# A fused attention and MLP kernel: the order of its first batch's steps, one chunk's place, and two loads moved

## The chip, the cores and the metric

The kernel runs on one core of one Trainium2 chip. The core has a matrix engine (PE), a vector engine (DVE), a scalar engine (ACT), GpSimd (POOL) and a fifth (SP) that here only issues DMAs. Each works through its own queue of instructions in order; semaphores tie the queues together. The metric is the time of one execution in microseconds, here the median of three runs.

## The reference, cut to what matters

```python
def _attn_ref(q, k, v, g_q, g_k):            # (8, 12, 448, 64) each
    rmsnorm = lambda x, g: x / np.sqrt(np.mean(x * x, axis=-1, keepdims=True) + 1e-06) * g
    q_n, k_n = rmsnorm(q, g_q), rmsnorm(k, g_k)
    scores = np.matmul(q_n, k_n.transpose(0, 1, 3, 2)) / np.sqrt(q.shape[-1])
    attn = np.exp(scores - np.max(scores, axis=-1, keepdims=True))
    attn = attn / (np.sum(attn, axis=-1, keepdims=True) + 1e-09)
    return np.matmul(attn, v)

def _moe_ref(x, w_in, w_out):                # (3584, 768), (768, 2048), (2048, 768)
    h = x @ w_in
    g = 0.5 * h * (1.0 + np.tanh(np.sqrt(2.0 / np.pi) * (h + 0.044715 * h * h * h)))
    return g @ w_out
```

The output of attention, with heads and positions swapped, is the input x of the two GEMMs.

## The kernel before

The eight batches are worked through one after the other. A batch's q and k come in three chunks of four heads each. Chunk c holds the head pairs 2c and 2c + 1, and `loads(b, c)` asks for it on SP with six DMAs: two of q (224 KB each), two of k's main part (192 KB each) and two of k's last 64 positions (32 KB each). The destination is a place in the pool `rawqk`, which has four. v comes per batch on POOL in three DMAs: `load_v(b, 0)` is the main part (576 KB as bf16), `load_v(b, 1)` and `load_v(b, 2)` are the last positions of two halves of the heads (48 KB each). W_in comes on POOL in two halves (1,536 KB each as bf16), W_out in four quarters (768 KB each).

A head pair goes through these steps: squares, their sums, 1/sqrt, the normed copy in bf16, a transpose on PE into PSUM, a copy from there into `qT` or `kT`, scores on PE, exponentials on ACT, sums of the exponentials on PE, their reciprocals on DVE (through two 32 x 32 transposes), the product with v on PE, and its scaling into `xT`. The first GEMM (L391, with `win`) turns `xT` into 16 blocks of hidden values, GELU runs on ACT, and the second GEMM (L418, with `wout`) makes rows of the output.

For batches 1 to 7 the attention of one batch is interleaved with the second GEMM of the batch before it, which fills PE. The first batch has nothing to fill with. Its instructions, and the preparation of batch 1 beside them, are written as a list of steps, `FRONT` (from L708), which `front` (from L623) turns into instructions one after another. Scheduling by the compiler is off, so each engine's queue has its instructions in the order in which the list names them. A step's name has a number and, for some, an engine after a colon: A for ACT, D for DVE, P for POOL.

- `sq0` to `sq5`, `sk0` to `sk5`: squares of q and k of head pair i (L181 on ACT, L183 on the others). `tq`, `tk`: their sums on DVE (L198). `rs`: 1/sqrt on ACT for a pair (L204, L207). `nq`, `nk`: normed copies (L221).
- `tpq`, `tpk`: transposes on PE (L233, L240). `cq`, `ck`: the copies out of PSUM (L248 to L259).
- `s0` to `s20`: scores, seven tiles per chunk (L302 for the one with k's last positions of both pairs, L312 for the others). `e0` to `e20`: their exponentials (L316), one ACT instruction each. Scores alternate between two places in PSUM, after `U` among three.
- `su`: the sums of the exponentials (L349, into `o`); `st`, `rc`, `rb`: their reciprocals (L356, L360, L364). `xp`: the product with v (L349, into `ox`); `xt`: the scaled result into `xT` (L374).
- `ma`, `mc`, `md`: the first GEMM, for the head pairs 0 to 3, 4 and 5 of the hidden blocks 0 to 5, and from `md3` on for all six. `g`: GELU. Blocks 0 to 7 read the first half of W_in, which makes `md4` the first that reads the second.
- `z`: matmuls of zeros, so many as the number says.
- `L10`, `L11`, `L12`: `loads(1, c)`. `v0`, `v1`, `v2`: v of batch 0; `V`: v of batch 1; `w0`, `w1`: W_in; `o0` to `o3`: W_out.
- `Sq`, `Sk`, `Tq`, `Tk`: squares and sums of a whole chunk of batch 1. `Rs`, `Nq`, `Nk`, `Tp`, `TP`, `Cq`, `Ck`: as above, for batch 1's first two chunks; batch 1's third is transposed by DMA later.

Before the list come the loads of batch 0. In the kernel before, two places of `rawqk` are then passed over without being filled. A DMA on SP also waits, in both kernels, until the one issued eight before it has landed, because their semaphores are used in turn.

Of the kernel before, what the change touches and what calls it, by code (L numbers as in the profile page):

```python
# [8 lines left out]
F32 = mybir.dt.float32  # L9
# [7 lines left out]
def kernel(  # L17
# [12 lines left out]
    B, H, S, D = q.shape  # L30
# [8 lines left out]
    P = 112  # L39
    NQ = S // P  # L40
    NK = 3
    NS = 7
    HP = H // 2
    CH = 4
# [7 lines left out]
    rawqk = ctx.enter_context(tc.tile_pool(name="rawqk", bufs=4))  # L52
# [29 lines left out]
    gcol = consts.tile([128, 1], F32)  # L82
# [3 lines left out]
    shift = consts.tile([128, 1], F32)  # L86
# [22 lines left out]
    def load_q(b, c):  # L109
        t = rawqk.tile([P, CH, NQ, D], F32, tag="rawq", name="rawq")  # L110
        raws["q", b, c] = t
        return [
            lambda j=j: nc.sync.dma_start(
                t[:, 2 * j:2 * j + 2],
                q[b, head(c, j):head(c, j) + 2].rearrange("h (p t) d -> p h t d", t=NQ),
            )
            for j in range(2)
        ]
# [6 lines left out]
    def load_k(b, c):  # L125
        t = rawqk.tile([128, 2, NS, D], F32, tag="rawk", name="rawk")
        raws["k", b, c] = t

        def main(j):
            h = head(c, j)  # L130
            nc.sync.dma_start(
                t[:, :, 4 * j:4 * j + NK],
                k[b, h:h + 2, :SM].rearrange("a (p t) d -> p a t d", t=NK),
            )

        def last(j):
            h = head(c, j)
            nc.sync.dma_start(t[own(j), :, NK], k[b, h:h + 2, SM:].rearrange("a p d -> p a d"))
        return [lambda: main(0), lambda: main(1), lambda: last(0), lambda: last(1)]

    def loads(b, c):
        lq, lk = load_q(b, c), load_k(b, c)
        for go in (lq[0], lk[0], lq[1], *lk[1:]):
            go()
# [19 lines left out]
    def sq_tile(n, flat):  # L164
        if n == "q":
            return flat[:P].rearrange("p (h t d) -> p h t d", h=CH, t=NQ)
        return flat[:, :2 * NS * D].rearrange("p (a s d) -> p a s d", a=2, s=NS)
# [29 lines left out]
    def total(b, c, n, j=None):  # L197
        nc.vector.reduce_sum(stat(ssq[b % 3], b, c, n, j), view(n, sqs[n, b, c], j), axis=AX.X)  # L198

    def rsqrt(b, c=slice(0, NCH), at=slice(0, NU)):  # L200
        if b not in rinvs:
            rinvs[b] = smp.tile([128, NCH, NU], F32, tag="rinv", name="rinv")
        lg = smp.tile([128, NCH, NU], F32, tag="lg", name="lg")
        nc.scalar.activation(  # L204
            lg[:, c, at], ssq[b % 3][:, c, at], AF.Ln, scale=1.0 / D, bias=eps
        )
        nc.scalar.activation(rinvs[b][:, c, at], lg[:, c, at], AF.Exp, scale=-0.5)  # L207
# [124 lines left out]
    def bank():  # L332
        return ps_o.tile([128, 512], F32, tag="o", name="o")
# [223 lines left out]
    nc.scalar.preload_act_table_set(EXP_SET)  # L557
    loads(0, 1)
    loads(0, 2)

    for _ in range(2):
        rawqk.tile([P, CH, NQ, D], F32, tag="rawq", name="rawq")
        rawqk.tile([128, 2, NS, D], F32, tag="rawk", name="rawk")
    nc.vector.memset(eps, 1e-6)
    nc.vector.memset(ones, 1.0)
    nc.vector.memset(rows, 1.0)
# [10 lines left out]
    free = g.rearrange("p f s -> p (f s)")  # L577
    for i, (n, c) in enumerate((n, c) for c in range(NCH) for n in "qk"):
        sqs[n, 0, c] = sq_tile(n, free[:, i * 2048:(i + 1) * 2048].bitcast(F32))

    def w_in_part(i, n):
        m = d_ff // n
        nc.gpsimd.dma_start(
            win[:, :, i * m:(i + 1) * m],
            moe_w_in[:, i * m:(i + 1) * m].rearrange("(c p) f -> p c f", p=128),
        )
# [34 lines left out]
    def front(step):  # L621
        what, _, eng = step.partition(":")
        name, i = what.rstrip("0123456789"), what[len(what.rstrip("0123456789")):]  # L623
        i, eng = int(i or 0), ENG.get(eng)
        c, j = i // 2, i % 2
        n = name[-1]
        if name in ("sq", "sk"):
            square(0, c, n, eng, ("pair", j))
        elif name in ("tq", "tk"):
            total(0, c, n, j)  # L630
        elif name == "rs":
            rsqrt(0, c, slice(14 * j, 14 + 16 * j))
        elif name in ("nq", "nk"):
            normed(0, c, n, j, eng)
        elif name in ("tpq", "tpk"):
            tps[n, i] = trans(0, i, n, turn[0], name)
        elif name == "cq":
            place_q(0, i, tps["q", i], eng)
        elif name == "ck":
            place_k(0, i, tps["k", i], eng)  # L640
        elif name == "U":
            third()
        elif name == "gcol":
            gains()
        elif name == "shift":
            shifts()
        elif name == "s":
            exps[i] = scores(0, *TILES[i])
        elif name == "e":
            exps[i]()  # L650
        elif name == "z":
            hp, m = divmod(i, 100)
            if hp not in sums_at:
                sums_at[hp] = bank()
            idle(m, sums_at[hp][:, :S])
        elif name == "su":
            pair_products(0, i, 0, sums_at.get(i))
        elif name == "st":
            recip_in()
        elif name == "rc":  # L660
            recip()
        elif name == "rb":
            recip_out(i)
        elif name == "xp":
            pair_products(0, i, 1, ps_m.tile([128, 512], F32, tag="mm", name="ox"))
        elif name == "xt":
            pair_x(0, i)
        elif name == "v":
            load_v(0, i)
        elif name == "w":  # L670
            w_in_part(i, 2)
        elif name == "V":
            load_v(1, i)
        elif name == "o":
            w_out_part(i // 2, slice(i % 2 * nf // 2, (i % 2 + 1) * nf // 2))
        elif name == "L":
            loads(*divmod(i, 10))
        elif name in ("Sq", "Sk"):
            square(1, i, n, eng)
        elif name in ("Tq", "Tk"):  # L680
            total(1, i, n)
        elif name == "Rs":
            rsqrt(1, slice(0, 2))
        elif name in ("Nq", "Nk"):
            normed(1, i // 10, n, i % 10, eng)
        elif name == "Tp":
            tps["Q", i] = trans(1, i, "q", ps_o, "o")
            tps["K", i] = trans(1, i, "k", ps_m, "mm")
        elif name == "TP":
            tp = place("tp").rearrange("p a s -> p (a s)").bitcast(BF16)  # L690
            tps["Q", i], tps["K", i] = (
                trans(1, i, n, tp[:, 1024 * a:1024 * (a + 1)]) for a, n in enumerate("qk"))
        elif name == "Cq":
            place_q(1, i, tps["Q", i], eng)
        elif name == "Ck":
            place_k(1, i, tps["K", i], eng)
        elif name in ("GELU", "EXP"):
            nc.scalar.preload_act_table_set(EXP_SET if name == "EXP" else GELU_SET)
        elif name in ("ma", "mc", "md"):
            fs = [2 * i, 2 * i + 1] if i < 7 else [i + 7]  # L700
            cs = {"ma": range(4), "mc": [4], "md": [5] if i < 3 else range(HP)}[name]
            mm1(0, fs, cs, act=False)
        elif name == "g":
            gelu(0, [2 * i, 2 * i + 1] if i < 7 else [i + 7])
        else:
            raise ValueError(step)

    FRONT = """  # L708
        sq0:A tq0 sk0:A tk0 sq1:P gcol rs0 shift nq0:P tq1 sk1:A tk1 tpq0 sq2:A v0 nk0:D rs1 cq0:D
        tpk0 tq2 sk2:A z3 v1 ck0:A tk2 v2 s0 nk1:D rs2 s1 w0 nq1:D e0 tpk1 sk3:D w1 tpq1 e1 s2 tk3  # L710
        z5 sq3:P ck1:D e2 cq1:D nk2:P tq3 s3 sq4:A s4 nq2:D rs3 tpk2 e3 tq4 nq3:P tpq2 z1 ck2:D e4
        cq2:D s5 nk3:D su0 e5 sk4:D L10 s6 tk4 sq5:P tpq3 e6 st0 tpk3 s7 sk5:P tq5 rs4 su1 rc0 e7
        rb0 nk4:P s8 ck3:D nq4:P s9 e8 st1 tpk4 cq3:D xp0 e9 ck4:D tk5 tpq4 xt0 s10 rs5 s11 cq4:D
        e10 xp1 nq5:P rc1 rb1 e11 s12 nk5:P xt1 su2 e12 L11 L12 s13 st2 tpq5 e13 tpk5 s14 rc2
        Sk0:P xp2 ck5:D e14 rb2 s15 xt2 su3 cq5:A Sq0:P e15 U Tk0 s16 xp3 e16 st3 s17 rc3 Tq0 s18
        e17 z403 rb3 e18 s19 su4 xt3 e19 s20 st4 xp4 e20 o0 rc4 rb4 ma0 GELU o1 xt4 Sq1:P su5 xp5
        V0 V1 st5 V2 Sk1:P rc5 mc0 rb5 ma1 xt5 Tq1 o2 o3 md0 mc1 Tk1 g0 md1 ma2 g1 EXP mc2 md2 md3
        Rs0 GELU Nq00:D Nk00:D Sk2:D g2 Tp0 md4 g3 Nk01:D Sq2:D Ck0:A Cq0:A Nk11:D md5 g4 Nq01:D
        Tq2 Nk10:P Nq10:P Tk2 Tp1 g5 Nq11:P md6 Ck1:D Cq1:A md7 g6 TP2 Ck2:D Cq2:D md8 TP3 Ck3:D
        Cq3:D g7 g8  # L720
"""
    for step in FRONT.split():
# [147 lines left out]
```

## Time and profile before

| | |
|---|---|
| runs shown | 431.62, 427.21, 426.42 us; median 427.21 us |
| profiled execution | 429.53 us, span 427.8 us |
| mean granted PE clock over the span | 0.992 |
| PE busy | 410.6 us, 96% of the span |
| ACT / DVE / POOL busy | 296.8 / 279.0 / 133.7 us |
| HBM read / written | 45.61 MB / 11.01 MB |
| first GEMM starts / first matmul of L418 | 41.08 us / 64.32 us from the span's start |

The span runs from the first to the last instruction, and the execution's own time includes what lies around it. Busy time of PE is counted with the modelled end of each matmul, so a busy PE is not PE at its peak. Rows of the page that have 40 digits show the span in 40 slices of 10.7 us, each digit the busy share in tenths; PEclk is the granted clock in tenths of full speed.

### The profile page before, as it was taken

The page shows a single profiled execution, that of the slowest core. Times are in us where ns is not written, and L with a number is a line of the kernel's source. Part 1 is how long each engine was busy: PE and PEld are TensorE (multiplying, and loading weights), DVE is VectorE, ACT ScalarE, POOL GpSimd, SP SyncE. Part 2 cuts the span into 40 slices and gives each one's busy share as a digit, 9 for nine tenths or more (in the row PEclk, how much of TensorE's full clock was granted, in tenths as well). Part 3 has the DMA queues.
Part 4 walks back from the last instruction along what each step waited for, and adds up shares of the span by engine and source line. Part 5 has one row for each costly group of instructions (what it writes and reads, how often), then busy time and mean ns, then how long its engine had stood idle before and what let it go on. Part 6 is the DMA issues. An engine that isn't in the chain of part 4 may idle for free.

```text
span 427.8 us, 9133 instructions
## 1 busy us (share of the span) xinstructions
PE 410.6 (96%) x3733; PEld 232.7 (54%) x3733; DVE 279.0 (65%) x452; ACT 296.8 (69%) x400; POOL 133.7 (31%) x139
## 2 busy tenths in 40 slices
PE   7697999999999999999999999999999999999996
PEld 2232555565555655556555655556555655556563
DVE  5985676798769856787468836787387742683010
ACT  5786659678898678776877668776777558774300
POOL 6737660016000375009520375008430370000000
PEclk9988999999999999999999999999999999999999
DMA  8999998954991098915992097925972061120022
GB/s 194 222 225 231 203 199 158 220 152 100 174 251 41 2 181 202 167 53 116 196 181 73 14 201 142 188 61 104 199 103 71 10 124 38 43 72 2 0 76 74
DMA packets 96298, 54.15 MB, mean 127 GB/s; under 512 B 63744, under 2 KB 91264, under 8 KB 96256
## 3 DMA queue, kind: packets, MB, share of 16 engines
q1 hardware_dynamic: 71392, 41.67, 42.9%
q0 software_dynamic: 24544, 11.80, 21.1%
q8 instruction: 29, 0.48, 0.5%
q10 hardware_dynamic: 320, 0.10, 0.1%
q14 instruction: 13, 0.11, 0.1%
HBM read 45.61 MB, written 11.01 MB: 132 GB/s over the span
## 4 chain that ended last, share of the span: by engine, by line
PE 81%; DMA 7%; ACT 5%; DVE 5%; issue 1%; SPq 1%; POOL 0%; DVEq 0%; ACTq 0%; POOLq 0%
PE o L418 33%; PE hh L391 25%; PE o L349 10%; DMA rawk<-in_k_dram 7%; PE sc L312 6%; PE h L391 4%; PE sc L302 1%; ACT g L400 1%; ACT ex L316 1%; DVE ss L198 1%; DVE sq L183 1%; ACT exr L316 1%; DVE es L328 1%; ACT sq L181 1%; DVE st L356 1%
## 5 line engine op out<-in xcount | busy, mean ns | idle before, releaser
L418 PE MATMUL o<-wout,g 128*64 128x384 bf16 (+1 forms) x1664 | 157.8, 326 | 0.0
L316 ACT ACTIVATE ex<-sc,shift 128x896 bf16<-128x896 f32 x144 | 136.2, 1013 | 6.4 <-PE sc L312 6.4
L391 PE MATMUL hh<-xT,win 128*64 128x448 bf16 (+1 forms) x924 | 133.2, 353 | 0.1
L418 PEld LDWEIGHTS <-g 128*64 128x64 bf16 (+1 forms) x1664 | 98.7, 109 | 49.1 <-issue 3.8
L391 PEld LDWEIGHTS <-win 128*64 128x64 bf16 (+1 forms) x1062 | 86.2, 105 | 59.1 <-issue 3.6
L400 ACT ACTIVATE g<-hh 128x896 bf16<-128x896 f32 x56 | 49.4, 916 | 48.7 <-PE hh L391 48.7
L198 DVE TENSOR_REDUCE ss<-sq 128x14 f32<-128x896 f32 (+2 forms) x43 | 47.4, 1124 | 30.4 <-ACT sq L181 18.5
L440 ACT COPY osb<-o 128x384 f32<-128x384 f32 x51 | 24.7, 484 | 49.2 <-PE o L418 49.1
L727 POOL COPY mark<-es 1x1 bf16<-1x1 bf16 x6 | 1.1, 178 | 170.2 <-DVE es L330 170.2
L356 DVE STREAM_TRANSPOSE st<-o 128x448 f32<-128x448 f32 x48 | 31.1, 648 | 28.2 <-PE o L349 28.1
L221 POOL TENSOR_TENSOR nrmq<-rawq,rinv 112x512 bf16<-112x512 f32 x36 | 38.8, 1093 | 6.0 <-ACT rinv L207 6.0
L312 PE MATMUL sc<-qT,kT 64*128 64x448 bf16 x288 | 39.4, 358 | 1.3 <-ACT exr L316 0.8
L330 DVE TENSOR_TENSOR es<-ex 128x896 bf16<-128x896 bf16 x42 | 26.3, 627 | 17.6 <-ACT ex L316 17.6
L221 POOL TENSOR_TENSOR nrmk<-rawk,rinv 128x384 bf16<-128x384 f32 (+1 forms) x34 | 35.4, 1055 | 5.0 <-issue 3.4
L349 PE MATMUL o<-ex,vb 128*64 128x448 bf16 x252 | 31.2, 353 | 1.2 <-DVE st L356 1.2
L364 DVE STREAM_TRANSPOSE rb<-rc 128x448 f32<-128x448 f32 x48 | 30.9, 645 | 1.6
L274 DVE TENSOR_SCALAR kT<-kT,gcol 128x896 bf16<-128x896 bf16 x19 | 21.8, 1146 | 13.4 <-DMA kT<-nrmk 13.4
L328 DVE TENSOR_TENSOR es<-es,exr 64x896 bf16<-64x896 bf16 x42 | 26.0, 618 | 3.0 <-ACT exr L316 1.6
L330 DVE TENSOR_TENSOR es<-es,ex 128x896 bf16<-128x896 bf16 x42 | 25.6, 609 | 2.6 <-ACT ex L316 0.7
L374 DVE TENSOR_TENSOR xT<-o,rb 128x448 bf16<-128x448 f32 x42 | 25.9, 616 | 0.7
L316 ACT ACTIVATE exr<-sc,shift 128x896 bf16<-128x896 f32 x24 | 24.5, 1019 | 0.6 <-PE sc L302 0.5
L312 PEld LDWEIGHTS <-kT 64*128 64x128 bf16 x288 | 10.1, 94 | 25.1 <-issue 19.3
(79 smaller groups left out, 333.3 us busy)
## 6 DMA issues: line engine op xcount, KB each, us to landing
rawq<-in_q_dram SPq DMA_DIRECT2D x48, 224.0 KB, 4.3
rawk<-in_k_dram SPq DMA_DIRECT2D x48, 192.0 KB, 4.6
vb<-in_v_dram POOLq DMA_DIRECT2D x8, 576.0 KB, 9.3
win<-in_moe_w_in_dram POOLq DMA_DIRECT2D x2, 1536.0 KB, 24.8
wout<-in_moe_w_out_dram POOLq DMA_DIRECT2D x4, 768.0 KB, 15.0
out_dram<-osb SPq DMA_DIRECT2D x7, 336.0 KB, 3.5
out_dram<-osb SPq DMA_DIRECT2D x8, 288.0 KB, 2.7
out_dram<-osb SPq DMA_DIRECT2D x8, 240.0 KB, 2.7
```

The lines of the kernel that those rows point to most:

```text
L198: nc.vector.reduce_sum(stat(ssq[b % 3], b, c, n, j), view(n, sqs[n, b, c], j), axis=AX.X)
L221: eng.tensor_mul(dst.rearrange("p t a d -> p a t d"), view(n, raws[n, b, c], j), r.to_broadcast(list(r.shape) + [D]),)
L312: nc.tensor.matmul(sc[:, a, :S], kT[r, c, 4 * j + t], qT[b][r, hp], start=True, stop=True,)
L316: return lambda: nc.scalar.activation(dst, sc[:, :, :S], AF.Exp, scale=scale, bias=shift)
L328: nc.vector.tensor_add(es[p], es[p], exrs[b, hp // 2][p])
L330: nc.vector.tensor_add(es, ex[:, 0] if t == 1 else es, ex[:, t])
L349: nc.tensor.matmul(o[a * D:(a + 1) * D], w(a), e[:, a], start=(i == 0), stop=(i + 1 == len(steps)),)
L356: nc.vector.transpose(oas["st"].rearrange("p a b -> p (a b)"), oas[0])
L364: nc.vector.transpose(oas["rb", hp], oas["rc"].to_broadcast([128, S // 32, 32]))
L391: nc.tensor.matmul(h[i * m:(i + 1) * m, j, :S], win[:, c // 2 + NCH * (c % 2), f * 128 + i * m:f * 128 + (i + 1) * m], xT[b][:, c], start= ...
L400: nc.scalar.activation(g[:, fs[0]:fs[0] + len(fs), (b % 2) * S:(b % 2 + 1) * S], hs1[fs[0]][:, :, :S], AF.Gelu_apprx_tanh)
L418: nc.tensor.matmul(o[j * m:(j + 1) * m, :HD], g[:, f, i * 128 + j * m:i * 128 + (j + 1) * m], wout[:, f, half * HD:(half + 1) * HD], start ...
```

## The change

There are three parts. `loads(1, 0)` stands directly behind `loads(0, 2)`, and the two places that were passed over are gone, so that batch 1's chunk 0 takes the fourth place of `rawqk`, chunk 1 takes the place of batch 0's chunk 0 and chunk 2 that of chunk 1. Of v, `v1` and `v2` stand ahead of `v0`. And the list has a new order: it moves steps of batch 0 and of the preparation of batch 1, gives some of them to other engines, puts `w0` and `w1` behind more of them, and has other counts of zero matmuls.

```diff
     loads(0, 1)
     loads(0, 2)
-
-    for _ in range(2):
-        rawqk.tile([P, CH, NQ, D], F32, tag="rawq", name="rawq")
-        rawqk.tile([128, 2, NS, D], F32, tag="rawk", name="rawk")
+    loads(1, 0)
...
+    NW = 2
...
-            w_in_part(i, 2)
+            w_in_part(i, NW)
...
-        sq0:A tq0 sk0:A tk0 sq1:P gcol rs0 shift nq0:P tq1 sk1:A tk1 tpq0 sq2:A v0 nk0:D rs1 cq0:D
-        tpk0 tq2 sk2:A z3 v1 ck0:A tk2 v2 s0 nk1:D rs2 s1 w0 nq1:D e0 tpk1 sk3:D w1 tpq1 e1 s2 tk3
-        z5 sq3:P ck1:D e2 cq1:D nk2:P tq3 s3 sq4:A s4 nq2:D rs3 tpk2 e3 tq4 nq3:P tpq2 z1 ck2:D e4
-        cq2:D s5 nk3:D su0 e5 sk4:D L10 s6 tk4 sq5:P tpq3 e6 st0 tpk3 s7 sk5:P tq5 rs4 su1 rc0 e7
-        rb0 nk4:P s8 ck3:D nq4:P s9 e8 st1 tpk4 cq3:D xp0 e9 ck4:D tk5 tpq4 xt0 s10 rs5 s11 cq4:D
-        e10 xp1 nq5:P rc1 rb1 e11 s12 nk5:P xt1 su2 e12 L11 L12 s13 st2 tpq5 e13 tpk5 s14 rc2
-        Sk0:P xp2 ck5:D e14 rb2 s15 xt2 su3 cq5:A Sq0:P e15 U Tk0 s16 xp3 e16 st3 s17 rc3 Tq0 s18
-        e17 z403 rb3 e18 s19 su4 xt3 e19 s20 st4 xp4 e20 o0 rc4 rb4 ma0 GELU o1 xt4 Sq1:P su5 xp5
-        V0 V1 st5 V2 Sk1:P rc5 mc0 rb5 ma1 xt5 Tq1 o2 o3 md0 mc1 Tk1 g0 md1 ma2 g1 EXP mc2 md2 md3
-        Rs0 GELU Nq00:D Nk00:D Sk2:D g2 Tp0 md4 g3 Nk01:D Sq2:D Ck0:A Cq0:A Nk11:D md5 g4 Nq01:D
-        Tq2 Nk10:P Nq10:P Tk2 Tp1 g5 Nq11:P md6 Ck1:D Cq1:A md7 g6 TP2 Ck2:D Cq2:D md8 TP3 Ck3:D
+        sq0:P sk0:A tq0 tk0 sq1:P gcol rs0 shift nq0:P tq1 sk1:A nk0:P tk1 tpq0 cq0:A sq2:D v1
+        tpk0 rs1 z5 tq2 v2 sk2:A ck0:D nq1:P sq3:A tk2 s0 s1 tq3 rs2 v0 tpq1 e0 nk1:D z1 nk2:D L11
+        tpk1 e1 s2 cq1:D sk3:P z1 ck1:D e2 s3 nq2:D tpk2 tk3 sk4:P e3 tpq2 s4 ck2:D sq5:P cq2:D
+        rs3 s5 tk4 su0 e4 nk3:P tq5 e5 s6 st0 nq3:P tpk3 rc0 e6 s7 ck3:D sq4:P L12 tpq3 rb0 e7 s8
+        cq3:D su1 w0 tq4 e8 s9 sk5:D xp0 rs4 st1 w1 e9 s10 rc1 nq4:P xt0 e10 s11 rb1 xp1 nk4:D e11
+        tk5 s12 tpk4 xt1 e12 tpq4 s13 ck4:D xp2 cq4:D rs5 e13 s14 nk5:D su2 nq5:P e14 tpk5 st2 s15
+        Sq0:P ck5:A tpq5 s16 rc2 e15 su3 cq5:D rb2 U e16 s17 xt2 Sk0:P st3 xp3 e17 rc3 rb3 s18 s19
+        xt3 e18 su4 Tk0 e19 xp4 st4 s20 rc4 ma0 rb4 o0 e20 xt4 GELU o1 Tq0 mc0 su5 xp5 st5 V0 V1
+        V2 rc5 ma1 rb5 xt5 md0 ma2 o2 o3 g0 Sq1:A Sk1:P mc1 md1 mc2 Tq1 g1 md2 md3 EXP Tk1 Rs0
+        GELU md4 Nq00:D Nq01:D g2 Nk00:D Nq11:D g3 Tp0 Nk11:D md5 Nk01:P g4 Ck0:D Cq0:A Nq10:P
+        Nk10:P Tp1 g5 md6 Sk2:D Ck1:A Cq1:D Sq2:P Tk2 md7 g6 Tq2 TP2 Ck2:D Cq2:D md8 TP3 Ck3:D
         Cq3:D g7 g8
```

## The prediction

> **What bounds the kernel now.** I read the page first, then the chain of work in order of time, then each engine's timeline up to 66 us.
>
> ```profile
> PE   7697999999999999999999999999999999999996
> PEclk9988999999999999999999999999999999999999
> DMA  8999998954991098915992097925972061120022
> ...
> PE 81%; DMA 7%; ACT 5%; DVE 5%; issue 1%; SPq 1%; POOL 0%; DVEq 0%; ACTq 0%; POOLq 0%
> ```
>
> One slice is 10.7 us. From slice 5 on PE is full, so every microsecond that the first four slices lose stays lost. The chain puts a number on it: its 7% DMA (29 us) all lies ahead of 34 us. In the chain by time (start, length, what):
>
> ```profile
> 9.31 6.88 DMA rawk<-in_k_dram
> 16.19 0.02 issue
> 16.21 16.88 DMA rawk<-in_k_dram
> ...
> 33.21 1.69 POOL sq L183
> 34.90 0.02 issue
> 34.92 1.09 DVE ss L198
> 36.01 0.57 DVE st L356
> 36.58 0.04 issue
> 36.62 1.28 PE o L212 x3
> ```
>
> The transfer issued at 16.21 is the last 32 KB of batch 1's chunk 0. It lands at 33.09, because W_in (issued on POOL at 10.66) shares the DMA engines with it. The square Sk0 waits for it, the total Tk0 for Sk0, and behind Tk0 in DVE's queue stands st3, a step of batch 0 whose result PE needs. ACT shows the price (start, length, then the wait ahead of it):
>
> ```profile
> 35.03 1.00 ACT L316 ACTIVATE ex<-sc,shift 128x896 bf16<-128x896 f32 x1
> 38.42 1.01 ACT L316 ACTIVATE ex<-sc,shift 128x896 bf16<-128x896 f32 x1 [2.40 <-PE sc L312]
> 40.31 1.01 ACT L316 ACTIVATE ex<-sc,shift 128x896 bf16<-128x896 f32 x1 [0.88 <-PE sc L312]
> ```
>
> These are e18, e19 and e20. After e20 PE has the first GEMM and nothing else to lose: ma0 starts at 41.08, the first fill matmul of the next stage (L418) at 64.32, and PE is busy 21.39 of the 22 us from 42 to 64. So two pieces count: the exponentials' queue up to e20, and the 23.2 us from ma0 to the fills.
>
> **The exponentials' queue, before.** e0 starts at 11.26, e20 ends at 41.32: 30.06 us. The waits ahead of ACT's instructions in that stretch are 1.58, 0.34, 1.01, 1.01, 0.50, 2.40 and 0.88, together 7.72; the last two, 3.28, come from the late load. Work: 22.34.
>
> **The same queue, after.** Between e0 and e20 stand the same 21 exponentials, three rs and one copy (ck5 for cq5); sq4 (0.62) goes to POOL. Work: 21.7.
>
> e0 stands behind rs2, and that waits for a DVE queue with more in it. Counted from tk1 (8.96 in the trace of before): sq2 0.61, tq2 0.62, ck0 0.33, tk2 0.48, tq3 0.62 with about 0.1 of hand-over gives 11.7; rs2 takes 0.55; e0 starts at 12.3, **1.0 later** than now. What goes to POOL in front costs nothing: sq0 on POOL (1.04 for 0.63) delays rs0 by 0.5, but nq0 waits until 7.2 for sq1, whose load lands at 6.09; nk0 on POOL (0.83 for 0.55) starts at 8.2 instead of 8.87.
>
> Waits between e0 and e20: none would give an end at 12.3 + 21.7 = 34.0; all of today's except the two of the late load (4.44) give 38.4. I walked the new list queue by queue (a step starts when its engine and inputs are free, durations from the rows of 0 to 66 us): waits of 2.0 are left. Walked the same way, today's list comes out 0.6 us early, so I take 2.6: **e20 ends at 36.6, 4.7 us earlier**. The walk finds fewer waits for a reason seen in the trace: nq1 now runs on POOL at 10.3 to 11.4 and frees DVE. Today it is this row:
>
> ```profile
> 11.72 2.24 DVE L221 TENSOR_TENSOR nrmq<-rawq,rinv 112x512 bf16<-112x512 f32 x1
> ...
> 16.48 0.68 DVE L221 TENSOR_TENSOR nrmq<-rawq,rinv 112x512 bf16<-112x512 f32 x1
> ```
>
> The same instruction takes 0.68 alone and 2.24 beside POOL's W_in issues and its sq3. The new list has 13 products on POOL and 7 on DVE for batch 0 (today 11 and 7), so such pairs remain; today's others cost 0.8 (nk3) and 0.9 (sk4).
>
> [...]
>
> **Batch 1's first chunk.** On SP nothing moves: its six issues are the 19th to 24th DMAs in both kernels, with the same waits, and run from 12.34 today. What changes is its company, since W_in moves past sk3, sk4, sq5, nk3, nq3 and sq4 in POOL's queue: about 11.4 + 1.2 (v's issue) + 1.5 + 1.0 + 1.2, then nk3 at 16.9 behind rs3 and three products of 1.0 each, hence 20.2 instead of 10.66. Four chunks of 896 KB and v's 672 KB are 4.36 MB; at the page's 220 GB/s from 2.5 us on they are in at about 22.5. Sq0 and Sk0 reach POOL's head at 28. The wait of 4.46 us there goes, and Tk0 no longer stands before a late load. What is late next is ACT itself.
>
> **v.** Its last tokens go first and the main part follows nk0 and nq1: issued at 11.3, not 8.15. Issue to landing was 9.3 to 14.4 for the three such loads, 10.8 for this one: landing at 20.6 to 22.1 (14.4 is behind W_out). xp0 can start at 21.3. Cost 0 to 0.8 on PE, 0.4 taken by ACT at most; it is within the 2.6.
>
> **W_in.** The two halves landed at these distances from their issues (shortest, middle, longest):
>
> ```profile
> DMA to landing us min/median/max: 20.5/24.8/29.2
> ```
>
> 10.66 + 20.5 = 31.2 and 11.48 + 29.2 = 40.7: 9.5 us a half, and the first began when v's last part had landed (9.35 + 11.4 and 10.01 + 11.8). Issued at 20.2 and beginning when v is in, the first half lands at 22.1 + 9.5 = 31.6 at the earliest; with today's whole 20.5 at 40.7 at the latest. Nearest are rows in which it queues only behind v, so I take 32 to 35. ma0 wants it at 41.1 - 4.7 = 36.4. The second half, 9.5 later (42 to 45), is first read by md4, at about 47. Chunks 1 and 2 of batch 1 then share with W_in: at the 54 GB/s that a chunk got beside it (917 KB from 16.2 to 33.1), they land at about 39 to 42 and 46 to 50; Tk1 wants its one by 44.5, Sk2 by 50. W_out ends the same line as now: 64 us, the first half at 53 to 54 (52.7 now), wanted at 59.
>
> **From ma0 to the fills.** Same 96 matmuls of L391, same transposes: 23.2 us in both. Sq1 moves to ACT between g0 and g1 (about 1.1 us, PE has ma2 and mc1 meanwhile); Sk2 and Sq2 leave the start of DVE's queue, which lets md5's neighbours Tp0 and Tp1 come earlier; I count nothing for either. Everything behind the fills keeps its order and its lengths.
>
> **Clock.** The granted clock was 0.55 from 22.5 to 25 and 0.54 from 37.5 to 40, each time after PE had waited 1.8 and 2.2 us. In the walk no wait over 1.1 us is left ahead of ma0, so no drop is counted; one drop put into the walk costs 0.2 to 1.3. [...]
>
> **Sum.** Fills start at 64.3 - 4.7 = 59.6; the span goes from 427.8 to 423.1, the profiled execution's own time from 429.53 to 424.8. The median shown (427.21) is 2.3 under that execution; with the same 4.7 off: **422.5 us**.
>
> **Rivals.**
> 1. *W_in takes the place of the late load* (slower). If the first half lands at 40.7, the latest bound, ma0 waits 40.7 - 36.4 = 4.3 us on PE with su5 and xp5 behind it, the clock halves for 3.4 us after (1.7 lost), and e20's gain is used up: 4.7 - 4.3 - 1.7 = 1.3 slower, **428.5**. It costs from a landing at 36.4 on, and turns the sign at 36.4 + 3.0 = 39.4. For it: W_in waited 20.5 us even when issued early. Against: most of that was v, ahead of it in POOL's queue, now over by then. 0.12.
> 2. *DVE and POOL hold each other up.* Two or three more overlaps at 0.8 to 1.6 us on the way to e10 leave 2 of the 4.7: **425.2**. 0.18.
> 3. *The chunk comes no earlier.* SP's order is unchanged and the DMA row is full in both; then nothing is gained but sq4's place: **427**. Against: the bytes ahead of it are over by 22.5. 0.05.
> 4. *ACT without waits.* e20 at 34.0, W_in in time: 7.3 off, **419.9**. Against: the e's still need PSUM turns and cq/ck steps. 0.15.
>
> The forecast (421 to 424) has 0.50. The range, 419 to 428, leaves out the slower rival and the far end of the fourth. 2% is 8.5 us, about what a measurement of this kernel tells from no change: faster by more, under 418.7, needs rival 4 and more from the GEMM stretch (0.07); slower by more, over 435.8, needs W_in at 47 or later (0.03); within, 0.90.
>
> **What would show it.** The idle before sq L183 on POOL for a rawk load (4.5 us) gone; W_in issued near 20 and landing 12 to 15 us later for its first half; e0 at 12.3, e20's end at 36 to 37; ma0 at 35.5 to 37, the first L418 at 59 to 60; no half clock between 20 and 40. A wait of L391 for win would make the first rival right; DVE rows of L221 over 1.5 us, the second. The prediction is wrong altogether if the stage behind the fills changes length, which I take as fixed.

## The result, and the profile after

The changed kernel takes **425.63 us** (median of 20 executions, 423.86 to 428.23), the kernel before 427.95 us (20 executions, 425.1 to 431.95): a ratio of 0.9941, 95% interval 0.9916 to 0.9965, so it is 2.3 us faster, 0.6%. The forecast was 422.5, that is 4.7 us faster than the median shown. Sign and range hold; the gain is half of the forecast, and the time 3.1 us off. One profiled execution below, the second of the kernel before (432.46 us, more than 1.5% above the fastest of its twelve), is a slow one, and no conclusion rests on it alone.

The profiled execution after took 427.94 us, span 426.2, the second longest of the 20. The page of after, the same rows (40 slices of 10.7 us, tenths) and the chain by engine:

```profile
PE   6798999999999999999999999999999999999995
PEclk9699999999999999999999999999999999999999
DMA  7999999926991199816992197915972051120022
...
PE 67%; issue 12%; DMA 6%; DVE 5%; POOL 4%; ACT 2%; SPq 2%; POOLq 0%; DVEq 0%
```

PE's first four slices are hardly fuller than before: 6, 7, 9, 8 tenths against 7, 6, 9, 7; and the granted clock has a 6 in the second slice, where before had two 8s in the third and fourth. The chain of after, in order of time (start, length, what), shows another bound:

```profile
13.03 0.67 DVE ss L198
13.71 3.77 DVE nrmk L221 x2
...
23.38 15.20 DMA win<-in_moe_w_in_dram
38.62 2.07 PE hh L391 x10
...
62.01 2.07 PE o L418 x23
```

The late load of batch 1's chunk 0 is gone from it: the last piece landed at 21.8 (33.09 before). In its place stand two products on DVE and W_in. ACT's timeline (start, length, then the wait ahead) has e2 and e20:

```profile
17.26 1.01 ACT L316 ACTIVATE ex<-sc,shift 128x896 bf16<-128x896 f32 x1 [1.76 <-PE sc L312]
...
37.44 1.01 ACT L316 ACTIVATE ex<-sc,shift 128x896 bf16<-128x896 f32 x1 [0.34 <-PE sc L312]
```

Of the waits of 2.40 and 0.88 ahead of e19 and e20, 0.34 is left, as good as forecast, but e0 starts at 13.61, e20 ends at 38.44 (before 41.32), ma0 starts at 38.62 and the fills at 61.94: 2.38 us earlier than before, where 4.7 was forecast. DVE's timeline shows what came in front:

```profile
5.98 2.17 DVE L598 TENSOR_TENSOR gcol<-grow 64x1 f32<-64x1 f32 x2
8.18 0.77 DVE L599 TENSOR_SCALAR gdiag<-ident,gcol 64x64 bf16<-64x64 bf16 x1
...
13.63 3.85 DVE L221 TENSOR_TENSOR nrmk<-rawk,rinv 128x512 bf16<-128x512 f32 x2
```

The two products of 64 x 1 numbers take 0.33 where nothing stands beside them; here 2.17, beside sq1 and nq0 on POOL (6.09 to 8.13). nk1 and nk2 take 3.85 beside sk3, sk4 and sq5. And W_in's two halves, by the view of its tile (us from issue to landing: shortest, middle, longest), with PE's first use of it:

```profile
DMA to landing us min/median/max: 15.2/18.5/21.8
```

```profile
38.62 2.07 PE L391 MATMUL hh<-xT,win 128*128 128x448 bf16 x10 [1.23 <-DMA win<-in_moe_w_in_dram]
```

From ma0 to the fills (the first matmul of L418) 23.3 us pass (23.2 forecast), and from there to the end of the last matmul of L418 359.9 (359.3 before). So what was won lies ahead of ma0, and of the 2.38 us 0.5 are lost again behind the fills.

### The profile page after: what moved, and what is told of

It is laid out like the page before. It is cut to its first block, busy times and chain, and to the rows that moved or that the text cites. A ratio compares the mean times of both kernels' runs of the same rounds, so it can differ in the third digit from the quotient of the medians.

```text
span 426.2 us, 9116 instructions
## 1 busy us (share of the span) xinstructions
PE 410.4 (96%) x3728; PEld 233.7 (55%) x3728; DVE 281.1 (66%) x452; ACT 296.1 (69%) x398; POOL 133.7 (31%) x141
## 4 chain that ended last, share of the span: by engine, by line
PE 67%; issue 12%; DMA 6%; DVE 5%; POOL 4%; ACT 2%; SPq 2%; POOLq 0%; DVEq 0%
PE o L418 27%; PE hh L391 21%; PE o L349 9%; PE sc L312 5%; DMA win<-in_moe_w_in_dram 4%; PE h L391 3%; POOL nrmq L221 1%; PE sc L302 1%; POOL nrmk L221 1%; DMA rawk<-in_k_dram 1%; DMA rawq<-in_q_dram 1%; DVE nrmk L221 1%; DVE ss L198 1%; POOL sq L183 1%; ACT ex L316 1%
## 5 line engine op out<-in xcount | busy, mean ns | idle before, releaser
L418 PE MATMUL o<-wout,g 128*64 128x384 bf16 (+1 forms) x1664 | 157.8, 326 | 0.0
L391 PE MATMUL hh<-xT,win 128*64 128x448 bf16 (+1 forms) x924 | 133.4, 353 | 1.4 <-DMA win<-in_moe_w_in_dram 1.2
L418 PEld LDWEIGHTS <-g 128*64 128x64 bf16 (+1 forms) x1664 | 99.0, 109 | 48.8 <-issue 3.8
L391 PEld LDWEIGHTS <-win 128*64 128x64 bf16 (+1 forms) x1062 | 86.1, 105 | 60.5 <-issue 3.5
L221 POOL TENSOR_TENSOR nrmk<-rawk,rinv 128x384 bf16<-128x384 f32 (+1 forms) x34 | 33.3, 994 | 10.5 <-PE hh L391 7.2
L349 PE MATMUL o<-ex,vb 128*64 128x448 bf16 x252 | 31.2, 353 | 1.6 <-DVE st L356 1.5
L274 DVE TENSOR_SCALAR kT<-kT,gcol 128x896 bf16<-128x896 bf16 x19 | 22.9, 1210 | 14.2 <-DMA kT<-nrmk 14.2
L183 POOL TENSOR_TENSOR sq<-rawq 112x1024 f32<-112x1024 f32 x8 | 16.0, 1997 | 27.6 <-DMA rawq<-in_q_dram 24.0
## 6 DMA issues: line engine op xcount, KB each, us to landing
vb<-in_v_dram POOLq DMA_DIRECT2D x8, 576.0 KB, 10.7
```

The costliest lines, as they stand in the source:

```text
L221: eng.tensor_mul(dst.rearrange("p t a d -> p a t d"), view(n, raws[n, b, c], j), r.to_broadcast(list(r.shape) + [D]),)
L349: nc.tensor.matmul(o[a * D:(a + 1) * D], w(a), e[:, a], start=(i == 0), stop=(i + 1 == len(steps)),)
L391: nc.tensor.matmul(h[i * m:(i + 1) * m, j, :S], win[:, c // 2 + NCH * (c % 2), f * 128 + i * m:f * 128 + (i + 1) * m], xT[b][:, c], start= ...
L418: nc.tensor.matmul(o[j * m:(j + 1) * m, :HD], g[:, f, i * 128 + j * m:i * 128 + (j + 1) * m], wout[:, f, half * HD:(half + 1) * HD], start ...
```

## The experiments

Each kernel was timed beside the kernel before on the same chip. The median of before differs: 429.44, 431.32, 429.38 and 429.95 us in the four groups below, each on another chip. The changed kernel was run again in the second group only. "Fills" is the first matmul of L418 in the profiled execution.

Theory: the gain is the late load's, and what is missing of the forecast is lost in front, where DVE's `gcol` (2.17 us for 0.33) and its products nk1 and nk2 (3.85) are held beside POOL's. Rivals: W_in's landing bounds ma0; or the named parts (the place, v's order) do the work; or the forecast's base was wrong.

**First group: the parts apart.** sq0 back on ACT in the changed kernel, so that nothing on POOL stands beside `gcol`:

```diff
-        sq0:P sk0:A tq0 tk0 sq1:P gcol rs0 shift nq0:P tq1 sk1:A nk0:P tk1 tpq0 cq0:A sq2:D v1
+        sq0:A sk0:A tq0 tk0 sq1:P gcol rs0 shift nq0:P tq1 sk1:A nk0:P tk1 tpq0 cq0:A sq2:D v1
```

> The changed kernel with one engine put back: sq0 on ACT, not on POOL. Hold-up theory: in the changed kernel tq0 ends 0.5 us later, so DVE's two 64x1 products (gcol) start at 5.98, just before POOL's sq1 and nq0 (6.09 to 8.13), and are held until 8.15 (2.17 us, 0.33 before the change). With sq0 on ACT gcol takes about 0.3, gdiag 0.23, e0 starts at about 12.2 rather than 13.6, and the fills start 1.2 to 1.8 us earlier than 62.0; ratio to the kernel before 0.989 to 0.992. W_in theory (ma0 waits for W_in, whatever comes before): e0 comes earlier, but ma0 only as far as W_in's issue on POOL does; if that stays at 23.4, the fills stay at 62.0 and the ratio at 0.994.

Measured: 425.21 us, ratio 0.9898 (0.9859 to 0.9937); fills 58.42. DVE's timeline of this kernel:

```profile
5.33 0.33 DVE L598 TENSOR_TENSOR gcol<-grow 64x1 f32<-64x1 f32 x2
...
12.09 1.15 DVE L221 TENSOR_TENSOR nrmk<-rawk,rinv 128x512 bf16<-128x512 f32 x2
```

and PE's:

```profile
22.62 0.76 PE L349 MATMUL ox<-ex,vb 128*64 128x448 bf16 x6 [2.36 <-DMA vb<-in_v_dram]
```

Both hold-ups are gone, e0 starts at 11.8 and e20 ends at 35.68. But now PE is early enough to wait for v: its main part, issued at 11.39 behind the last tokens, lands at 22.58. The fills come 3.5 us earlier than in the changed kernel's execution above, twice what was expected; part of that is the execution above, a long one of its kernel (its second, below, has the fills at 60.26).

W_in's two issues earlier in POOL's queue, all else as changed:

```diff
-        tpk1 e1 s2 cq1:D sk3:P z1 ck1:D e2 s3 nq2:D tpk2 tk3 sk4:P e3 tpq2 s4 ck2:D sq5:P cq2:D
+        tpk1 e1 s2 cq1:D sk3:P z1 ck1:D e2 s3 nq2:D tpk2 tk3 sk4:P e3 tpq2 s4 ck2:D sq5:P w0 w1 cq2:D
...
-        cq3:D su1 w0 tq4 e8 s9 sk5:D xp0 rs4 st1 w1 e9 s10 rc1 nq4:P xt0 e10 s11 rb1 xp1 nk4:D e11
+        cq3:D su1 tq4 e8 s9 sk5:D xp0 rs4 st1 e9 s10 rc1 nq4:P xt0 e10 s11 rb1 xp1 nk4:D e11
```

> The changed kernel with W_in's two issues put behind sq5 on POOL, ahead of nk3, nq3 and sq4 (about 17.1 instead of 23.4). W_in theory: the first half lands at 31 to 34, the 1.2 us in which L391 waits for win go, ma0 starts at about 37.2, the fills at about 60.7; ratio 0.990 to 0.992. Hold-up theory: the exponentials' queue is unchanged (e20 ends at 38.4, within 0.3), and ma0, which needs only xt3, gains up to the same 1.2; anything beyond 1.2 would speak against both. Cost to look for: batch 1's chunk 0 shares with W_in again and lands after 25 (21.8 in the changed kernel); Sq0 does not ask before 31.

Measured: 425.44 us, ratio 0.9902 (0.9864 to 0.9941); issued at 16.60, first half landed at 33.04, no wait at ma0 (35.52), fills 59.38. `gdiag` took 2.02 us here instead of 0.23. The numbers expected were missed: e20 ends at 36.64, the fills are 2.6 us earlier instead of 1.2, which was to speak against both theories, and chunk 0 is in by 22.08, not after 25. Against the changed kernel's second execution the fills are 0.9 earlier, and e20's end too. The wait for W_in can go, and the median hardly moves (425.44; 425.63 and 425.77 for the changed kernel on other chips).

The kernel before with one thing changed, W_in's issues behind sk5:

```diff
-        tpk0 tq2 sk2:A z3 v1 ck0:A tk2 v2 s0 nk1:D rs2 s1 w0 nq1:D e0 tpk1 sk3:D w1 tpq1 e1 s2 tk3
+        tpk0 tq2 sk2:A z3 v1 ck0:A tk2 v2 s0 nk1:D rs2 s1 nq1:D e0 tpk1 sk3:D tpq1 e1 s2 tk3
...
-        cq2:D s5 nk3:D su0 e5 sk4:D L10 s6 tk4 sq5:P tpq3 e6 st0 tpk3 s7 sk5:P tq5 rs4 su1 rc0 e7
+        cq2:D s5 nk3:D su0 e5 sk4:D L10 s6 tk4 sq5:P tpq3 e6 st0 tpk3 s7 sk5:P w0 w1 tq5 rs4 su1 rc0 e7
```

> The kernel before with one move alone: W_in's two issues behind sk5 on POOL (about 20.7 instead of 10.7). Late-load theory: batch 1's chunk 0 lands by 23 (33.1 before), the waits of 2.8 us on DVE for Sk0 and of 2.25 us on PE for st3 go, e20 ends about 3.3 us earlier than 41.3, the fills start at 61 to 62; 2.3 to 3.3 us faster, ratio 0.992 to 0.995, as much as the whole change. The rival, that the change's gain comes from the new order and engines: W_in comes late here too, lands at about 36 and takes the place of the late load, ratio 0.998 to 1.002.

Measured: 425.23 us, ratio 0.9907 (0.9871 to 0.9943), rather more than expected; chunk 0 in by 23.27, e20's end 37.02, fills 59.76. On POOL the square Sk0 follows at 28.51 without a wait. Its chain by time has no late load of k and no W_in:

```profile
7.67 3.35 DMA rawq<-in_q_dram
11.03 2.33 DVE nrmk L221
...
36.59 1.62 PE hh L391 x8
...
59.83 4.02 PE o L418 x48
```

The kernel before with the other two parts of the change, W_in left where it was:

```diff
-    for _ in range(2):
...
+    loads(1, 0)
...
-        sq0:A tq0 sk0:A tk0 sq1:P gcol rs0 shift nq0:P tq1 sk1:A tk1 tpq0 sq2:A v0 nk0:D rs1 cq0:D
-        tpk0 tq2 sk2:A z3 v1 ck0:A tk2 v2 s0 nk1:D rs2 s1 w0 nq1:D e0 tpk1 sk3:D w1 tpq1 e1 s2 tk3
+        sq0:A tq0 sk0:A tk0 sq1:P gcol rs0 shift nq0:P tq1 sk1:A tk1 tpq0 sq2:A v1 nk0:D rs1 cq0:D
+        tpk0 tq2 sk2:A z3 v2 ck0:A tk2 v0 s0 nk1:D rs2 s1 w0 nq1:D e0 tpk1 sk3:D w1 tpq1 e1 s2 tk3
...
-        cq2:D s5 nk3:D su0 e5 sk4:D L10 s6 tk4 sq5:P tpq3 e6 st0 tpk3 s7 sk5:P tq5 rs4 su1 rc0 e7
+        cq2:D s5 nk3:D su0 e5 sk4:D s6 tk4 sq5:P tpq3 e6 st0 tpk3 s7 sk5:P tq5 rs4 su1 rc0 e7
```

> The kernel before with the two named moves and without the new list: batch 1's chunk 0 asked for directly behind batch 0's in the fourth place, and v's last tokens ahead of its main part; W_in stays where it was. SP's order and waits for these six DMAs are the same, so the chunk lands at 32 to 34 as before and the stall behind Sk0 stays. Ratio 0.998 to 1.002. If the place or v's order were what brings the gain, the chunk would land by 25 and the ratio be below 0.997.

Measured: 428.2 us, ratio 0.9984 (0.9952 to 1.0015); W_in issued at 10.69, chunk 0's last piece landed at 31.87, e20's end 40.13, fills 63.99. POOL's timeline still has Sk0's wait:

```profile
31.99 1.68 POOL L183 TENSOR_TENSOR sq<-rawk 128x896 f32<-128x896 f32 x1 [3.45 <-DMA rawk<-in_k_dram]
```

So **two DMA issues moved in POOL's queue give what the whole change gives**, and the place and v's order give nothing that can be measured. The new list with W_in left at its early place was not run; what its other moves give by themselves is open.

**Second group: the hold-up in front.** The changed kernel once more, for a second profiled execution:

> The changed kernel itself once more, beside the next three on one chip. Hold-up theory: ratio 0.991 to 0.995, slower than the two kernels in which the hold of gcol and gdiag is taken away (by 0.002 to 0.005). W_in theory: no different from them.

Measured: 425.77 us, ratio 0.9875 (0.9833 to 0.9916). W_in was in at 36.52 and ma0 started at 36.56, after 0.08 us of idle PE; e0 12.89, e20's end 37.53, fills 60.26. `gdiag` was held, 2.07 us for 0.23. Then `gcol` moved ahead of tq0, so that sq0 stays on POOL:

```diff
-        sq0:P sk0:A tq0 tk0 sq1:P gcol rs0 shift nq0:P tq1 sk1:A nk0:P tk1 tpq0 cq0:A sq2:D v1
+        sq0:P sk0:A gcol tq0 tk0 sq1:P rs0 shift nq0:P tq1 sk1:A nk0:P tk1 tpq0 cq0:A sq2:D v1
```

> The changed kernel with gcol (and gdiag) ahead of tq0 on DVE, sq0 left on POOL: the hold taken away from its other side. Hold-up theory: gcol starts when grow has landed (about 5.2) and gdiag ends by 5.9, ahead of POOL's sq1 at 6.1; tq0, tk0 and rs0 come 0.5 to 1.0 later, nq0 0.5 later; e0 at 12.3 to 12.9 instead of 13.6, the fills 0.7 to 1.5 us earlier than the changed kernel's; ratio 0.989 to 0.993. W_in theory: ma0 and fills as in the changed kernel, ratio 0.994.

Measured: 425.3 us, ratio 0.9859 (0.9813 to 0.9904); `gcol` 0.34, e0 11.92, but PE waits 2.65 for v's main part (landed 22.93), fills 59.88. The other way round, W_in late in the kernel before as above, and sq0 on POOL:

```diff
-        sq0:A tq0 sk0:A tk0 sq1:P gcol rs0 shift nq0:P tq1 sk1:A tk1 tpq0 sq2:A v0 nk0:D rs1 cq0:D
+        sq0:P tq0 sk0:A tk0 sq1:P gcol rs0 shift nq0:P tq1 sk1:A tk1 tpq0 sq2:A v0 nk0:D rs1 cq0:D
```

> The kernel before with W_in later (behind sk5) and sq0 on POOL, that is the earlier one-move kernel with one more step changed. Hold-up theory: gcol or gdiag takes about 2 us beside POOL's sq1 and nq0, e0 starts 1 to 2.3 us later than 11.6, and as nothing waits for a late load any more, the fills come 0.7 to 2 us later than 59.8; ratio 0.992 to 0.996 against 0.9907 without it. If moving sq0 to POOL is free, as the prediction had it: 0.990 to 0.992.

Measured: 425.19 us, ratio 0.9859 (0.9818 to 0.99); `gcol` 1.08 and `gdiag` 0.99, e0 12.46 (11.61 with sq0 on ACT), fills 59.92 (59.76). So the hold-up comes with sq0 on POOL in this list as well; it costs e0 0.9 us, but the fills only 0.2, where 0.7 to 2 was expected, and the median nothing (425.19 against 425.23 on the other chip). Beside it on one chip the whole change had 425.77, so W_in's move alone gives at least as much there too. Last, sq0 on ACT and v's main part ahead of its last tokens:

```diff
-        sq0:P sk0:A tq0 tk0 sq1:P gcol rs0 shift nq0:P tq1 sk1:A nk0:P tk1 tpq0 cq0:A sq2:D v1
-        tpk0 rs1 z5 tq2 v2 sk2:A ck0:D nq1:P sq3:A tk2 s0 s1 tq3 rs2 v0 tpq1 e0 nk1:D z1 nk2:D L11
+        sq0:A sk0:A tq0 tk0 sq1:P gcol rs0 shift nq0:P tq1 sk1:A nk0:P tk1 tpq0 cq0:A sq2:D v0
+        tpk0 rs1 z5 tq2 v1 sk2:A ck0:D nq1:P sq3:A tk2 s0 s1 tq3 rs2 v2 tpq1 e0 nk1:D z1 nk2:D L11
```

> The changed kernel with sq0 on ACT and with v's main part ahead of its last tokens again (issued at about 8.9 instead of 11.4; the last tokens at about 10 and 11.5). With sq0 on ACT alone PE waited 2.4 us for vb, which landed at 22.6. Theory that v's order costs once the front is early: vb lands at 19.5 to 21, the wait falls below 1 us, e10 starts 1 to 2 us earlier than 23.9, the fills at 57 to 58; ratio 0.985 to 0.988. The rival, that W_in then sets the end: W_in's issue moves by less than e10, ma0 waits for win, and the ratio stays at 0.988 to 0.991.

Measured: 425.86 us, ratio 0.9866 (0.9823 to 0.9909). v's main part is in at 19.5, e0 starts at 11.29 and e20 ends at 33.78, 3.75 us earlier than in the changed kernel beside it (the fourth rival of the forecast had 34.0 there); and PE's timeline shows where that goes:

```profile
35.34 3.48 PE L391 MATMUL hh<-xT,win 128*128 128x448 bf16 x10 [2.61 <-DMA win<-in_moe_w_in_dram]
```

W_in landed at 35.29, the granted clock is halved for 3.4 us from 35.8, and the fills are at 60.29, not at the 57 to 58 of the theory.

**Third group: W_in's landing, and before once more.** The kernel above with W_in behind sq5:

```diff
-        tpk1 e1 s2 cq1:D sk3:P z1 ck1:D e2 s3 nq2:D tpk2 tk3 sk4:P e3 tpq2 s4 ck2:D sq5:P cq2:D
+        tpk1 e1 s2 cq1:D sk3:P z1 ck1:D e2 s3 nq2:D tpk2 tk3 sk4:P e3 tpq2 s4 ck2:D sq5:P w0 w1 cq2:D
...
-        cq3:D su1 w0 tq4 e8 s9 sk5:D xp0 rs4 st1 w1 e9 s10 rc1 nq4:P xt0 e10 s11 rb1 xp1 nk4:D e11
+        cq3:D su1 tq4 e8 s9 sk5:D xp0 rs4 st1 e9 s10 rc1 nq4:P xt0 e10 s11 rb1 xp1 nk4:D e11
```

> The changed kernel with three things put back or forward: sq0 on ACT, v's main part ahead of v's last tokens, and W_in issued behind sq5 instead of behind su1 and st1. Theory (three arrivals take turns as the last: the exponentials' start, v's main part, W_in's first half): e0 at 11.3, e20's end at 33.8 as in the run with v's main part first, W_in issued near 15.5 and its first half in by 31 to 33, so that the wait of 2.6 us at ma0 goes; ma0 at 33.5, fills at 57 to 58, the time 1.5 to 3 us under the changed kernel's 425.7, 423 to 424. Rival (the exponentials and PE's own work bound the front by now, or batch 1's chunks come late beside an earlier W_in): ma0 may come earlier, but the fills stay at 59 to 60.3 and the time at 425 to 426.

Measured: 424.81 us (423.64 to 426.86), ratio 0.9921 (0.9883 to 0.9959). W_in's first half is in at 30.96 and waited for by nobody, but e3 starts at 17.27, e20 ends at 36.58, fills 59.32; the theory's 423 to 424 us is missed. DVE's timeline has the reason:

```profile
11.68 4.19 DVE L221 TENSOR_TENSOR nrmk<-rawk,rinv 128x512 bf16<-128x512 f32 x2
```

The same two products, nk1 and nk2, took 1.15, 2.25, 2.26, 2.84 and 3.85 us in other runs of nearly this list. Next, W_in later, behind nq4, in the changed kernel:

```diff
-        cq3:D su1 w0 tq4 e8 s9 sk5:D xp0 rs4 st1 w1 e9 s10 rc1 nq4:P xt0 e10 s11 rb1 xp1 nk4:D e11
+        cq3:D su1 tq4 e8 s9 sk5:D xp0 rs4 st1 e9 s10 rc1 nq4:P w0 w1 xt0 e10 s11 rb1 xp1 nk4:D e11
```

> The changed kernel with W_in's two halves issued behind nq4 on POOL, about 2.7 us later. Theory (W_in's first half is what ma0 waits for in the changed kernel): issued at 24 to 26, landed at 39 to 41, PE waits 1 to 4 us for it at L391, ma0 at 39 to 41, fills at 62.3 to 64.4, the time 1 to 3 us over the changed kernel's 425.7, near 427 to 428.5. Rival (W_in is in time in the median execution and the exponentials set ma0): ma0 at 36.5 to 38.6, the time 425.5 to 426.

Measured: 427.23 us (424.9 to 430.25), ratio 0.9959 (0.9918 to 1.0). Issued at 26.05, landed at 38.49, and PE's timeline:

```profile
38.54 3.69 PE L391 MATMUL hh<-xT,win 128*128 128x448 bf16 x10 [2.01 <-DMA win<-in_moe_w_in_dram]
```

with the granted clock halved for 3.4 us behind it and the fills at 63.49. W_in binds when it is issued 2.7 us later than in the change, and then the single executions spread over 5.4 us again. The median is 1.5 us over the changed kernel's, which was not run on this chip; by the ratio (0.9959, against 0.9941 in the first comparison) that difference is within the noise.

The kernel before, unchanged:

> The kernel before, unchanged, for a second profiled execution of it. Theory (the late last 32 KB of batch 1's chunk 0 and a W_in issued near 10.7 are its habit, and what they cost varies from one execution to the next): the square Sk0 on POOL waits 3 to 6 us for a load that lands at 32 to 36, ACT waits 1.5 us or more twice ahead of e18 to e20, e20's end at 40 to 43, fills at 63 to 66. Rival (the profiled execution of before was an odd one): the load lands before 30, no such waits, e20's end at 38 or earlier.

Measured: 427.77 us, ratio to itself 0.9977 (0.9935 to 1.0019). Its profiled execution is the longest of its twelve, 432.46 us, with the dearest late load of those profiled. POOL's timeline, then PE's, then ACT's:

```profile
35.08 1.68 POOL L183 TENSOR_TENSOR sq<-rawk 128x896 f32<-128x896 f32 x1 [9.29 <-DMA rawk<-in_k_dram]
```

```profile
38.48 1.28 PE L212 MATMUL o<-zeros 128*128 128x448 bf16 x3 [7.68 <-DVE st L356]
```

```profile
40.29 1.01 ACT L316 ACTIVATE ex<-sc,shift 128x896 bf16<-128x896 f32 x1 [7.83 <-PE sc L312]
42.42 1.01 ACT L316 ACTIVATE ex<-sc,shift 128x896 bf16<-128x896 f32 x1 [1.12 <-PE sc L312]
```

The exponentials were 3.6 us earlier than in the first profiled execution (e16 at 29.41 against 32.97), and the end is 2.8 us later. From the landing of the last 32 KB to the fills it is 31.2 us in the first (33.09 to 64.32), 32.1 with the place and v's order changed (31.87 to 63.99) and 32.2 here (34.95 to 67.16). So **in the kernel before the landing sets the fills**. That a faster front then only waits longer is seen in this last execution alone.

**One product more moved**, in the kernel with v's main part first and W_in behind sq5:

```diff
-        tpk0 rs1 z5 tq2 v1 sk2:A ck0:D nq1:P sq3:A tk2 s0 s1 tq3 rs2 v2 tpq1 e0 nk1:D z1 nk2:D L11
+        tpk0 rs1 z5 tq2 v1 sk2:A ck0:D nq1:P sq3:A tk2 s0 s1 tq3 rs2 v2 tpq1 e0 nk1:D z1 nk2:P L11
```

> The kernel of the run with v's main part first and W_in behind sq5, with one product more moved: nk2 goes from DVE to POOL, ahead of sk3. Theory (in the run before it nk1 and nk2 took 4.19 us on DVE beside sk3, sk4, sq5 and W_in's issues on POOL, against 1.15 where they ran undisturbed, and this put e3 at 17.3): nk1 alone takes 0.7 on DVE, nk2 1.0 on POOL and is out by 13.5, e3 at 14 to 15, e20's end at 33.5 to 35, W_in issued near 16.5 and in by 32 to 33, ma0 at 33 to 34.5, fills at 57 to 58.5, the time 423 to 424. Rival (another pair of products, or the transfer of W_in, takes the place): e3 may come at 14 to 15, but ma0 stays at 35 to 36, fills at 59 to 60 and the time at 424.5 to 425.5.

Measured: 425.66 us (423.89 to 426.85), ratio 0.9913 (0.9881 to 0.9944); e3 at 14.19 as the theory has it, fills at 58.51 in the profiled execution, which was the shortest of its twelve. DVE's timeline:

```profile
11.54 0.82 DVE L221 TENSOR_TENSOR nrmk<-rawk,rinv 128x512 bf16<-128x512 f32 x1
...
13.26 3.34 DVE L221 TENSOR_TENSOR nrmq<-rawq,rinv 112x512 bf16<-112x512 f32 x1
```

nk1 is free, and the next product, nq2, is held by the same three squares of POOL: e6 ends at 21.05, which is 2 us later than in the run with v's main part first (19.08). The rival's mechanism holds: another pair takes the place, and the time is no shorter. In this short execution ma0 (34.65) and the fills come earlier than the rival had them.

## Why the prediction was right, and where it failed

The forecast was wrong in its size, 4.7 us where 2.3 were measured; the mechanism behind its sign was right.

**The late load: right, and enough for the whole gain.** Chunk 0 lands at 21.8 (22.5 forecast), Sk0 and Tk0 wait for nothing, the two waits ahead of e19 and e20 are gone but for 0.34. That this comes from W_in's company and not from SP's order is shown by the two runs that do one part each: 0.9907 and 0.9984.

**The step from the profiled execution to the median: wrong, and most of the error.** The prediction took the 4.7 us off 429.53, which gives 424.8, and then off the median shown, 427.21, which gives 422.5. That supposes that every execution of before has the same 4.7 us to lose. The runs show otherwise. Over the 106 executions of before timed here the median is 429.5, with half of them between 427.3 and 431.2; of the changed kernel's 26 half lie between 425.2 and 426.7. The spread goes with the granted clock, which the record lists for 86 of before: the 21 with 0.994 or more have a median of 427.3 us, the 40 under 0.99 one of 431.2; of the changed kernel 8 and 7 executions have 425.1 and 426.8. So the difference between the kernels is about 2.2 us among executions with an almost full clock and 4.4 among the others. In both profiled executions of before a half clock begins within the waits for the late load (36.39 and 33.6), so the load can bring both; which share of the spread is the landing's and which the clock's was not separated. With W_in moved and nothing else, nine executions lie within 424.66 to 426.31, where the kernel before on that chip had 426.0 to 432.47. So the short executions of before have less to lose; the three shown had a low median, with two of them short. The profiled execution, at 429.53, was by chance the typical one, and 424.8 is 0.9 from the 425.7 that the changed kernel's 26 executions have as their median. That the gain differs, 2.3 us in the first comparison and 5.5 in the second, on another chip, may have the same ground. What a short execution of before looks like inside was not profiled; that its chunk lands earlier is argued, not shown.

**The remaining 0.9 us: the front, as far as the profiled executions go.** In the second profiled execution, close to the median, the fills are at 60.26 (59.6 forecast). The step that failed is "What goes to POOL in front costs nothing". The prediction counted sq0 and nk0 by POOL's and ACT's queues alone and left out what they do to DVE: with sq0 on POOL, tq0 ends later, `gcol` and `gdiag` start when sq1 and nq0 are running, and are held 1.8 to 2.5 us together; e0 starts at 12.9 to 13.8 in all four executions where that happened in the changed list, 11.3 to 11.9 in the five where it did not, 12.3 forecast. The forecast's waits of 2.6 in the exponentials' queue stand against 3.1 in the first profiled execution (38.44 - 13.61 - 21.7).

**W_in: late at the far end.** Issued at 23.38 and 21.64, not 20.2, it landed at 38.58 and 36.52, not 32 to 35: nk3 and the two products ahead of it on POOL wait for rs3, which stands behind e3 on ACT, so nk3 starts at 20.39 and 18.66, not 16.9; and the landing comes 15.2 and 14.9 us after the issue. PE waits 1.23 us, and 0.08: rival 1's mechanism, with a price far from what it needs to turn the sign. Moving W_in's issues 2.7 us later shows that rival's slope as far as chips compare: 1.5 us on the median (427.23 against 425.7). Chunks 1 and 2 of batch 1, forecast for 39 to 42 and 46 to 50, are in by 27.1 and 37.1 (27.5 and 43.9 in the second execution): chunk 1's loads, asked for from 16.4 on, have little of W_in beside them. The 54 GB/s that this part used counted chunk 0 from its last issue; from its first, at 12.34, it is 44. Nothing waited for either chunk.

**Rival 2 gave 425.2, and its rows are there.** DVE's instructions up to 36 us ran longer than the shortest with the same tiles and shape in these four executions by 5.9 and 4.8 us in the two of the changed kernel, 3.6 and 1.6 in the two of before. What is not shown is that this is what the median lacks. Taking the first hold-up away moved e0 by 1 to 2.3 us in each of the runs above, and the medians were 425.21, 425.3 and 425.86: something else was last each time, v's main part (2.4 and 2.65 us), W_in (2.61) or the next product on DVE (4.19, 3.34). The forecast's "what is late next is ACT itself" is therefore wrong too. These arrivals and hold-ups stand close behind each other, and taking one away left the median within 0.5 us of the changed kernel's.

**v: cost 0 to 0.8, landing 20.6 to 22.1.** It landed at 24.97 and 24.4; PE waited nothing and 1.20 us, the second more than allowed for. **Clock: no drop counted, 10.2 us at half seen** (9.6 to 13.0 and 16.4 to 23.2), each stretch behind a wait of PE, 2.20 and 2.36 us, that comes from a hold-up which the prediction did not have. **From ma0 on** little moved: 23.3 us to the fills, 359.9 behind them.

No variant beats the changed kernel by more than the intervals allow: the lowest median is 424.81, with three things changed at once, and the simplest of them, the kernel before with two issues moved, has 425.23.

## What to carry to other kernels

When the thing removed is a wait for a transfer, look at the spread of the single executions before setting the median: where the time varies, the price read in one profiled execution is that execution's, and taking it off shorter ones promises too much. A DMA issue is part of the order too; here two issues moved in one queue gave what the whole change gave. And before handing a product to an idle engine, ask what the other engine runs in that same microsecond, not only whether its queue has room: with sq0 on POOL `gcol` took 2.17 us, with sq0 on ACT 0.33.

## What the runs showed of the hardware

**Which of the two engines waits differs from run to run, and a row of POOL instructions went through as one in some of them.** nq2 on DVE took 3.34 us from 13.26 while POOL ran three squares one after another from 13.23 to 16.04, and ended 0.56 behind the last. In the run with sq0 back on ACT nk1 and nk2 both went ahead of sk3 (12.09 to 13.24), and it was sk3 that took 1.65 us instead of 1.04. In the run with v's main part first and W_in behind sq5, sk3 came in between the two, and nk2 alone took 3.17 us, to 0.42 behind the end of sq5. So the same pair took 1.15 in one run and 4.19 in another, with nearly the same neighbours in the list. It is not always the whole row: in the changed kernel's second execution and in the run with v's main part first, nk2 ended 0.42 behind sk3, and sk4, the next on POOL, took 1.12 and 1.16 instead of 0.82. Where nk2 or nq2 was the one that took longer, it ended 0.42 to 0.56 us behind POOL's; sk3 ended 0.90 behind nk2. The start alone does not settle which it is: with sq0 back on ACT, nk2, recorded from 12.69, went ahead of sk3, recorded from 12.49. What settles it was not shown.

**The same length of wait was followed by a half clock in one execution and not in another.** In the kernel before, PE waited 1.77 us up to 14.02 and the granted clock stayed full; it waited 1.76 up to 22.33, and 3.41 us at half followed. So a wait of 1.8 us, one of the two that the prediction names ahead of a fall, had one behind it once in two. The wait of 2.36 us up to 16.23 in the changed kernel's first execution was followed by 6.83 us at half. The wait of 2.36 us for v with sq0 on ACT left the clock at full (the six matmuls behind it took 0.76 us), one of 2.65 at the same place (with `gcol` ahead) was followed by 3.41 us at half (1.33 us for the same six); waits of 2.61 and 2.01 for W_in came with 3.41 us at half (3.48 and 3.69 us for ten matmuls of L391, 2.07 in the changed kernel's first execution). What decides between the two outcomes was not shown.
